# A retention layer and a squared-ReLU FFN on one core: every engine's row of operations written down

## The chip, the core and the metric

One core of a Trainium2 chip runs the whole kernel in one launch. Time is device microseconds (us) of that core. Five engines with queues of their own work side by side: TensorE (PE, matmuls), VectorE (DVE), ScalarE (ACT), GpSimd (POOL) and SyncE (SP, which here only issues DMAs). Each takes its instructions strictly in the order in which they were put into its queue.

## What is computed

```python
gamma = 1.0 - 2.0 ** (-5.0 - np.arange(H))          # q, k, v: (4, 8, 768, 64)
for t in range(S):
    state = gamma * state + outer(k[:, :, t], v[:, :, t])
    y[:, :, t] = (1 / sqrt(64)) * q[:, :, t] @ state
x = y.transpose(0, 2, 1, 3).reshape(3072, 512)
h = np.maximum(x @ w_in, 0.0)                       # w_in (512, 2048)
out = (h * h) @ w_out                               # w_out (2048, 512), out (3072, 512)
```

Inputs and output are float32; the kernel's matmuls run in bf16.

## The kernel before

The 3072 tokens are 24 chunks of 128. Everything that the kernel does is written down as an *operation* with a name: `Plan.add` collects the name, the engine or engines that may do it, an assumed duration, and what it reads and writes. `Plan.schedule` then replays the operations on an assumed clock and returns one sequence; the instructions are put into the engines' queues in that sequence. So `schedule` decides the order on each queue, which of the four PSUM tiles (`fps`, here called banks) a group takes, and which of two `r` buffers a ReLU takes. No time of that replay is a measurement.

The operations, by name:

- `ldk m`, `ldq m`, `ldv m`: load of chunk m (chunks 0 to 3 in pairs, `TWIN`), SP. `ldwin n`, `ldwout n`: slices of the weights, SP. They land in float32 in four slots each.
- `ck m`, `cq m`, `cv m`, `cwin j.c`, `cwout j.c`: casts to bf16 (lines 518, 520, 522 by engine; cv multiplies by decay factors, line 728). ck, cq and the weight casts may run on ACT, DVE or POOL.
- `X m`: for chunks from 7 on, a transposing DMA of casted q and k into `qkT` (line 761), SP. For earlier chunks `Tk m`, `Tq m` transpose on PE into a bank and `Ek m`, `Eq m` read it out; chunk 6 is flipped inside a visit and read out by `E6`.
- `A`, `B`, `C`: scores, state sums, and values for the first four chunks in pairs. `V m.n`: a *visit*, the values of chunk m and the scores and sums of chunk n in one block of matmuls (lines 787 to 824); `V.5` has scores alone, `V4.` values alone. After it DVE makes `P n` (masked scores), `S n.0`, `S n.1` (states) and `Y m` (the FFN's input, `xt`). The scores of V m.n need X n.
- `F1.b.f`: first FFN product of block b (one or two chunks; `BLOCKS`), a group of matmuls into one bank (line 936). `R b.f` is its ReLU on ACT (line 943), which frees the bank; `Q b.f` its square, on ACT (line 950) or DVE (line 952).
- Second product: for chunks 0 to 3 plain, `F2.c.j` (line 1108), read out by `O c` on ACT, stored by `st c`. For chunks 4 to 23 in pairs c, c+1, by seven products instead of eight (Strassen's way): DVE makes sums of h (here `S1`, `S2`, `S5`, `S6`, `S7` with the pair's number) and of w_out (`WT i`), PE the products `M1.c` to `M7.c` (line 1032), and `e4`, `cc` (ACT), `t1`, `u1`, `w`, `c` (DVE, line 1050) put them together; the last pair has `c1`, `c2` in place of `c`. Two stores, `st c.1` (cc) and `st c.0` (w and c's tile), line 1084; the last pair has three, lines 1075 and 1077.

What sets the order before: at each step `schedule` takes, of all operations that could start on any engine, the one with the least key.

```python
                    key = (t, o["prio"], i)
                    if best is None or key < best[0]:
                        best = (key, i, eng)
```

`prio` comes from formulas (`urgency(m)`, `LAGS`, `WPRIO`, `dma_order`) or from the table `RANK`, the engine for many operations from the table `HOME`. All stores but st22.0 go to SP.

The queues that came out of this, from the first FFN product to the tenth chunk and at the end:

```
PE   ... B3 F1.0.0 F1.0.2 C2.0 C2.1 F1.0.4 Tq4 F1.1.0 F1.0.6 F1.1.2 F1.1.4 F1.1.6 F1.0.8 Tk4 F1.0.10 F1.1.8 F1.1.10
     V.4 F1.0.12 F1.0.14 F1.1.12 V4. F2.0.0 Tq5 F1.1.14 F1.2.0 F2.0.1 Tk5 F1.2.4 F1.2.8 F2.0.2 F2.1.0 F1.2.12 F2.1.1
     F2.1.2 F2.0.3 F2.1.3 V.5 F2.2.0 F2.2.1 F2.3.0 F2.3.1 V5.6 F2.2.2 F2.2.3 F1.3.0 F1.3.4 F1.3.8 V6.7 F1.3.12
     F2.3.2 F2.3.3 M3.4 V7.8 M4.4 ... M3.22 M4.22 M6.20 M7.20 M1.22 M5.22 M2.22 M7.22 M6.22
SP   ... ldwin5 ldv4 ldwout0 ldq5 ldwout1 ldk5 ldwout2 ldwout3 ldq6 ldv5 ldk6 ldv6 ldq7 ldk7 ldv7 ldk8 ldq8 st0 st1
     X7 ldv8 ldk9 X8 st2 ldq9 ldv9 ldk10 ldq10 ldv10 st3 X9 ...
ACT  ... cwin0.0 cwin0.2 cwin1.0 R0.0 cwin2.2 Q0.0 R0.2 Q0.2 cwin3.2 R0.4 R1.0 Q1.0 cwin4.3 R0.6 R1.2 Q0.6 R1.4 R0.8 ...
```

Of the kernel before, what the change touches and what calls it, by code (L numbers as in the profile page):

```python
# [11 lines left out]
BF16 = mybir.dt.bfloat16  # L12
# [6 lines left out]
class Plan:  # L19
# [14 lines left out]
    HOP = 0.15  # L34

# [5 lines left out]
    def add(self, name, eng, dur, reads=(), writes=(), fn=None, prio=0.0, lat=0.0, bank=None, after=(), count=0, slot=None, lock=()):  # L41
# [19 lines left out]
        if name in HOME:  # L61
            eng = {HOME[name]: eng[HOME[name]]}
        prio = RANK.get(name, prio)
        self.ops.append(dict(i=i, name=name, eng=eng, flex=flex, deps=sorted(deps), fn=fn,
                             prio=prio, lat=lat, bank=bank, count=count, slot=slot, lock=lock))
        return i

    def schedule(self, nbanks, max_open, nslots):
# [12 lines left out]
        for o in ops:  # L81
            for e in o["eng"]:
                eng_free.setdefault(e, 0.0)
                pool.setdefault(e, set())
                if left[o["i"]] == 0:
                    pool[e].add(o["i"])
# [15 lines left out]
        while done < n:  # L102
            best = None
            for eng, cand in pool.items():
                ef = eng_free[eng]
                for i in cand:
# [17 lines left out]
                    key = (t, o["prio"], i)  # L124
                    if best is None or key < best[0]:
                        best = (key, i, eng)
            assert best is not None, "no operation can be placed"
            (t, _, _), i, eng = best
            o = ops[i]
            for e in o["eng"]:  # L130
                pool[e].discard(i)
# [34 lines left out]
            else:  # L166
                if eng == "PE":
# [21 lines left out]
                    if any(before < x <= issued for x in range(self.BLOCK0 - self.AHEAD, issued + 1, self.BLOCK)):  # L189
# [14 lines left out]
                end[i] = t + dur + o["lat"]  # L204
# [15 lines left out]
            for u in users[i]:  # L220
                same = list(ops[u]["eng"]) == [eng] and not move
                ready_at[u] = max(ready_at[u], start[i] + dur if same else end[i] + self.HOP)
                left[u] -= 1
                if left[u] == 0:
                    for e in ops[u]["eng"]:
                        pool[e].add(u)
# [11 lines left out]
AHEAD = 4  # L238
WARM = 20.0
FILL = 0.215  # L240
WARMING = 18.4
PACE = 8
LEAD = 2
# [5 lines left out]
CVT = {'DVE': 0.69, 'POOL': 1.07}  # L249
TCAST = {'DVE': 0.43, 'ACT': 0.63, 'POOL': 0.64}  # L250
TEVAC = {'ACT': 0.6, 'DVE': 0.62}
NPAIR = 2
F2LAG = 3.5
F2WAIT = 4
LAST = [256, 128, 128]
CAST = {"k": {"DVE": 0.43, "ACT": 0.63, "POOL": 0.64}, "q": {"DVE": 0.43, "ACT": 0.63, "POOL": 0.64}}
WCAST = {"DVE": 0.43, "ACT": 0.63, "POOL": 0.64}
EVAC = {"ACT": 0.6, "DVE": 0.62}
WPRIO = {"in": -2.0, "out": 2.0, "sum": 3.0}
# [3 lines left out]
SQUARE = {"DVE": 0.7, "ACT": 0.63}  # L263
WSUM = {"DVE": 0.69}
ASUM = {"DVE": 0.69}
LAGS = {
    16: 4.0, 4: 10.75, 6: 18.25, 10: 2.25, 20: 1.75, 14: 3.0, 8: 2.25, 18: 3.0, 12: 1.75, 22: 2.0,
}
RELU = {"ACT": 0.6}
# [4 lines left out]
PAIRS_A = {"S1": ((0, 0), (1, 1), ALU.add, None), "S5": ((0, 0), (0, 1), ALU.add, None),  # L274
           "S2": ((1, 0), (1, 1), ALU.add, None), "S6": ((1, 0), (0, 0), ALU.subtract, (1, 0)),
           "S7": ((0, 1), (1, 1), ALU.subtract, (0, 1))}
HOME = {
    'cwin4.1': 'POOL', 'ck0.1': 'ACT', 'Eq2.0': 'ACT', 'cwout2.1': 'ACT', 'cwin4.2': 'DVE', 'cwout3.0': 'DVE',
    'S5.18': 'DVE', 'R12.14': 'ACT', 'R1.10': 'ACT', 'Q8.10': 'DVE', 'R6.0': 'ACT', 'ck10': 'POOL', 'R6.14': 'ACT',
    'Q9.4': 'ACT', 'ck20': 'POOL', 'cq13': 'POOL', 'Q10.14': 'ACT', 'R4.8': 'ACT', 'R11.0': 'ACT', 'R3.12': 'ACT',  # L280
    'R4.14': 'ACT', 'cq2.1': 'DVE', 'cwin5.0': 'DVE', 'Q4.2': 'ACT', 'Ek2.0': 'ACT', 'ck21': 'POOL', 'Q8.6': 'ACT',
    'S7.20': 'DVE', 'Q11.6': 'ACT', 'Q10.10': 'DVE', 'Ek2.1': 'DVE', 'cq16': 'ACT', 'R1.8': 'ACT', 'S2.4': 'DVE',
    'WT7.0': 'DVE', 'Q12.6': 'DVE', 'Q2.8': 'ACT', 'Q6.2': 'ACT', 'R0.10': 'ACT', 'cq9': 'POOL', 'Q3.4': 'ACT',
    'R7.4': 'ACT', 'ck11': 'DVE', 'R8.0': 'ACT', 'Q5.2': 'ACT', 'R7.10': 'ACT', 'ck15': 'POOL', 'S2.20': 'DVE',
    'R7.12': 'ACT', 'cq5': 'ACT', 'Q7.6': 'DVE', 'ck5': 'DVE', 'ck4': 'POOL', 'cwin0.2': 'ACT', 'Q10.8': 'DVE',
    'Q7.4': 'DVE', 'R3.4': 'ACT', 'Q7.14': 'ACT', 'R4.10': 'ACT', 'R8.6': 'ACT', 'WT7.1': 'DVE', 'R9.6': 'ACT',
    'Ek4': 'DVE', 'S2.6': 'DVE', 'Q4.14': 'ACT', 'cv2.1': 'DVE', 'R6.6': 'ACT', 'Q7.12': 'DVE', 'cwout1.1': 'POOL',
    'Q12.0': 'ACT', 'S6.6': 'DVE', 'Q7.0': 'ACT', 'cwin3.2': 'ACT', 'S2.12': 'DVE', 'S5.22': 'DVE', 'Ek0.1': 'DVE',
    'Q0.0': 'ACT', 'cq17': 'ACT', 'S1.22': 'DVE', 'R7.14': 'ACT', 'cq18': 'POOL', 'S7.18': 'DVE', 'R9.12': 'ACT',
    'S2.14': 'DVE', 'R6.4': 'ACT', 'R3.8': 'ACT', 'Q6.0': 'ACT', 'R0.6': 'ACT', 'cq0.0': 'ACT', 'R4.0': 'ACT',  # L290
    'cq0.1': 'POOL', 'R0.14': 'ACT', 'S6.16': 'DVE', 'cwin5.3': 'ACT', 'S7.4': 'DVE', 'R5.12': 'ACT', 'S7.16': 'DVE',
    'ck22': 'POOL', 'S1.6': 'DVE', 'Q1.8': 'ACT', 'Eq0.0': 'DVE', 'R5.10': 'ACT', 'ck8': 'ACT', 'Q9.10': 'ACT',
    'R8.10': 'ACT', 'cq22': 'POOL', 'S2.18': 'DVE', 'Q6.4': 'DVE', 'R11.14': 'ACT', 'Q9.12': 'DVE', 'Q3.12': 'DVE',
    'cq4': 'POOL', 'ck2.0': 'ACT', 'cwout1.3': 'POOL', 'R7.8': 'ACT', 'Q9.6': 'ACT', 'R10.2': 'ACT', 'WT4.1': 'DVE',
    'Eq2.1': 'ACT', 'Q11.2': 'DVE', 'Q7.2': 'ACT', 'cq19': 'POOL', 'R11.8': 'ACT', 'Q7.8': 'DVE', 'S6.22': 'DVE',
    'S7.14': 'DVE', 'Q3.0': 'ACT', 'Q11.10': 'DVE', 'cwin1.2': 'POOL', 'S0': 'ACT', 'R9.10': 'ACT', 'Q9.8': 'DVE',
    'ck9': 'POOL', 'cwin3.0': 'POOL', 'Q0.6': 'ACT', 'Ek0.0': 'DVE', 'R5.14': 'ACT', 'S6.4': 'DVE', 'Q5.6': 'DVE',
    'cwout1.0': 'DVE', 'R9.0': 'ACT', 'Eq5': 'DVE', 'R8.14': 'ACT', 'S1.8': 'DVE', 'S7.12': 'DVE', 'S7.6': 'DVE',
    'R6.10': 'ACT', 'R12.6': 'ACT', 'cwin2.2': 'ACT', 'R4.12': 'ACT', 'cwout2.2': 'POOL', 'Q8.4': 'ACT',
    'Q11.0': 'ACT', 'R10.14': 'ACT', 'Q5.10': 'ACT', 'R10.12': 'ACT', 'cwout0.0': 'DVE', 'S2.22': 'DVE',  # L300
    'R10.10': 'ACT', 'R11.12': 'ACT', 'Q10.0': 'ACT', 'Q11.12': 'DVE', 'cq21': 'POOL', 'S5.12': 'DVE', 'R8.2': 'ACT',
    'Q0.8': 'ACT', 'Q6.6': 'ACT', 'Q5.8': 'ACT', 'R2.8': 'ACT', 'S6.12': 'DVE', 'R7.6': 'ACT', 'Q7.10': 'ACT',
    'cwin4.3': 'ACT', 'Q0.14': 'DVE', 'R1.14': 'ACT', 'cwout3.3': 'ACT', 'R9.4': 'ACT', 'Q5.4': 'ACT', 'S6.18': 'DVE',
# [33 lines left out]
    'R11.0': 16.0, 'M2.4': 73.143, 'Q0.8': 4.0, 'M5.6': 89.857, 'R0.14': 2.75, 'Q5.6': 12.75, 'M5.16': 162.857,  # L337
    'V10.11': 63, 'X11': 1.5, 'S21.1': 17.0, 't1.18': 27.0, 'cq8': -11.0,
}
ORDER = (  # L340
    "k0 q0 v0 q2 k2 v2 i0 i1 i2 q4 i3 i4 k4 i5 v4 o0 q5 o1 k5 o2 o3 q6 v5 k6 v6 q7 k7 v7"
)

# [9 lines left out]
def kernel(  # L353
# [638 lines left out]
    def products(c0):  # L992
# [31 lines left out]
        def product(i, bank, half, bank_use):  # L1024
# [13 lines left out]
            if first:  # L1038
                op["op"] = pl.ops[k]
# [168 lines left out]
```

## Time and profile before

| what | us |
|---|---|
| three runs | 203.77, 204.69, 204.86; median 204.69 |
| the profiled execution: span from first to last instruction | 202.7 |
| what lies around the span, by the runs | 1.1 to 2.2 |
| PE busy, DVE busy, ACT busy, POOL busy | 192.8, 150.0, 130.3, 31.3 |
| first FFN product starts | 17.54 |
| visit V7.8 starts | 62.42 |
| last matmul group ends | 198.94 |
| granted TensorE clock | 1.00 in every slice |

The profiled execution has no run time of its own, so its span stands beside the runs. The profile has a page (busy shares, forty slices of the span, DMA queues, the chain of work that ended last, the costliest groups, the DMA issues) and views of the trace behind it: a timeline by engine, lists of waits, and the chain in order of time. A matmul row's length is modelled and overlaps the next; the distance from one group's start to the next is its pace.

### The profile page before, as it was taken

To read this page: it belongs to the slowest core of one execution; us is meant where nothing else is said; L and a number is where in the kernel's file an instruction comes from. 1 tells how busy PE (TensorE), PEld (TensorE's weight loads), DVE (VectorE), ACT (ScalarE), POOL (GpSimd) and SP (SyncE) were. 2 spreads that over 40 slices of the span, in tenths; PEclk is the share of its full clock that TensorE was granted. 3 is DMA by queue.
4 is the path that set the end of the run, shared out by engine and by line. 5 is a ranking of instruction groups with operands and counts; after the bars stand their busy time and mean duration, and the time that the engine had idled before them with its cause. 6 is when DMAs were issued, how large, how long until landed. Compare 5 with 4: busy or idle time off the path is not lost.

```text
span 202.7 us, 7020 instructions
## 1 busy us (share of the span) xinstructions
PE 192.8 (95%) x3032; PEld 159.4 (79%) x3032; DVE 150.0 (74%) x283; ACT 130.3 (64%) x229; POOL 31.3 (15%) x56
## 2 busy tenths in 40 slices
PE   8886999899989999999999999999999999999992
PEld 6554887664577888888888888888888888888881
DVE  3486449569849988969898888878998784934762
ACT  8565888788871883787975485569375873835210
POOL 6541252220102101310211012203010000000000
PEclk9999999999999999999999999999999999999999
DMA  5999999999999999999999999999676100111313
GB/s 159 290 314 320 348 344 330 361 246 210 236 191 219 231 247 212 205 234 186 148 240 165 261 211 218 178 222 194 143 145 97 48 17 3 52 52 55 102 55 105
DMA packets 97935, 38.46 MB, mean 190 GB/s; under 512 B 81008, under 2 KB 94320, under 8 KB 97904
## 3 DMA queue, kind: packets, MB, share of 16 engines
q1 hardware_dynamic: 97760, 37.89, 86.2%
q8 instruction: 23, 0.38, 0.8%
q10 hardware_dynamic: 144, 0.13, 0.2%
q14 instruction: 8, 0.07, 0.1%
HBM read 27.26 MB, written 6.29 MB: 166 GB/s over the span
## 4 chain that ended last, share of the span: by engine, by line
PE 75%; DMA 15%; SPq 5%; POOL 1%; DVE 1%; issue 1%; ACT 0%; DVEq 0%
PE fps L936 33%; PE fps L1032 29%; DMA kn<-in_k_dram 8%; PE fps L1108 6%; DMA wst<-in_moe_w_in_dram 4%; DMA qkT<-kqs 3%; SPq L910 3%; PE yy L787 2%; SPq L537 2%; PE yy L802 1%; PE sc L813 1%; PE sc L824 1%; POOL w_in L522 1%; DVE wu L1050 1%; POOL h L522 0%
## 5 line engine op out<-in xcount | busy, mean ns | idle before, releaser
L936 PE MATMUL fps<-xt,w_in 128*128 128x256 bf16 (+1 forms) x832 | 94.0, 264 | 1.6 <-ACT w_in L518 1.2
L936 PEld LDWEIGHTS <-w_in 128*128 128x128 bf16 x832 | 74.8, 98 | 11.5 <-ACT w_in L518 2.0
L943 ACT ACTIVATE r<-fps 128x512 f32<-128x512 f32 x96 | 56.4, 592 | 34.6 <-PE fps L936 28.6
L950 ACT ACTIVATE h<-r 128x512 bf16<-128x512 f32 x63 | 39.1, 627 | 1.4
L1032 PE MATMUL fps<-wst,h 128*128 128x256 bf16 x320 | 39.4, 273 | 0.0
L1032 PEld LDWEIGHTS <-h 128*128 128x128 bf16 x320 | 31.0, 98 | 3.9
L952 DVE TENSOR_TENSOR h<-r 128x512 bf16<-128x512 f32 x33 | 22.8, 705 | 8.7 <-ACT r L943 8.6
L1032 PEld LDWEIGHTS <-wst 128*128 128x128 bf16 x240 | 23.3, 98 | 2.8
L1007 DVE TENSOR_TENSOR wst<-h 128x1024 bf16<-128x1024 bf16 x30 | 19.4, 685 | 2.9 <-ACT h L950 2.6
L1032 PE MATMUL fps<-w_out,wst 128*128 128x256 bf16 x160 | 20.3, 273 | 0.0
L728 DVE TENSOR_TENSOR vs<-vn,vf 128x512 bf16<-128x512 f32 x20 | 13.8, 691 | 6.3 <-DMA vn<-in_v_dram 6.3
L889 DVE TENSOR_TENSOR xt<-yy,yf 128x512 bf16<-128x512 f32 x20 | 13.7, 687 | 3.5 <-PE yy L802 3.4
L522 POOL CAST kqs<-kn 128x512 bf16<-128x512 f32 x12 | 8.0, 666 | 51.0 <-DMA kn<-in_k_dram 32.3
L1108 PE MATMUL fps<-w_out,h 128*128 128x512 bf16 x64 | 15.0, 379 | 0.7 <-DVE w_out L520 0.7
L1007 DVE TENSOR_TENSOR h<-h 128x1024 bf16<-128x1024 bf16 x20 | 14.0, 729 | 0.2
L880 DVE TENSOR_TENSOR state<-sc,state 128x256 bf16<-128x256 f32 x33 | 13.8, 418 | 0.5
L867 DVE TENSOR_TENSOR pt<-sc,cmask 128x512 bf16<-128x512 f32 x20 | 13.6, 681 | 0.0
L522 POOL CAST kqs<-qn 128x512 bf16<-128x512 f32 x11 | 6.9, 626 | 42.9 <-DMA qn<-in_q_dram 30.6
L1050 DVE TENSOR_TENSOR wu<-fps,wu 128x512 f32<-128x512 f32 (+1 forms) x16 | 9.1, 572 | 5.0 <-ACT osb L1060 2.8
L1108 PEld LDWEIGHTS <-h 128*128 128x128 bf16 x64 | 5.9, 98 | 6.8 <-issue 0.8
L1060 ACT ACTIVATE osb<-fps 128x512 f32<-128x512 f32 x10 | 5.9, 594 | 8.3 <-PE fps L1032 8.3
L1050 DVE TENSOR_TENSOR osb<-fps,osb 128x512 f32<-128x512 f32 (+1 forms) x15 | 9.0, 601 | 2.6 <-PE fps L1032 1.7
(85 smaller groups left out, 173.4 us busy)
## 6 DMA issues: line engine op xcount, KB each, us to landing
qn<-in_q_dram SPq DMA_DIRECT2D x20, 256.0 KB, 5.1
kn<-in_k_dram SPq DMA_DIRECT2D x20, 256.0 KB, 5.6
vn<-in_v_dram SPq DMA_DIRECT2D x20, 256.0 KB, 5.2
out_dram<-osb SPq DMA_DIRECT2D x19, 256.0 KB, 3.3
wst<-in_moe_w_out_dram SPq DMA_DIRECT2D x4, 1024.0 KB, 10.1
wst<-in_moe_w_in_dram SPq DMA_DIRECT2D x4, 512.0 KB, 8.4
wst<-in_moe_w_in_dram SPq DMA_DIRECT2D x2, 1024.0 KB, 8.3
kn<-in_k_dram SPq DMA_DIRECT2D x2, 512.0 KB, 4.3
```

Source lines behind the costliest of these rows:

```text
L522: nc.gpsimd.tensor_copy(o, t)
L728: lambda: nc.vector.tensor_tensor(out=o[:], in0=t.rearrange("s (h d) -> s h d", h=H), in1=vf[:, i, :, None].to_broadcast([P, H, D]), op=AL ...
L880: f = lambda cc=cc, j1=j1, j0=j0: nc.vector.tensor_tensor(out=sts[j1][:], in0=cc, in1=sts[j0][:], op=ALU.add)
L889: lambda: nc.vector.tensor_tensor(out=xt[:, :, u * C : u * C + C].rearrange("s p (g t) -> s g p t", g=2), in0=yy[:, :, 0:256].rearrange("s ...
L936: nc.tensor.matmul(ps[:, u * n : u * n + n], lhsT=w_in_bf[j][:, cb, c * P : (c + 1) * P], rhs=xt[:, cb, cols], start=(cb == 0), stop=(cb = ...
L943: nc.scalar.activation(o, t, AF.Relu)
L950: nc.scalar.activation(hv, rv, AF.Square)
L952: (nc.vector if on == "DVE" else nc.gpsimd).tensor_tensor(out=hv, in0=rv, in1=rv, op=ALU.mult)
L1007: lambda on, o=a[name], x=a[x], y=a[y], op=op: (nc.vector if on == "DVE" else nc.gpsimd).tensor_tensor(out=o, in0=x, in1=y, op=op), prio=c ...
L1032: nc.tensor.matmul(ps[:, 256 * half : 256 * half + 256], lhsT=a[left][:, f], rhs=right(f), start=(first and f == 0), stop=True, skip_group ...
L1050: return lambda ps: nc.vector.tensor_tensor(out=o, in0=ps[:, lo:hi], in1=y, op=op)
L1108: nc.tensor.matmul(ps[:, 0:w], lhsT=h2[:, fb, u * C : u * C + C], rhs=w_out_bf[j][:, c, ns], start=(fb == 0), stop=(fb == NFB - 1))
```

## The change

The tables `HOME`, `RANK` and `ORDER`, `LAGS`, and all `prio` arguments go. A new table `TURNS` holds, for every engine, the full row of operation names, and `schedule` may place only the next name of a row; it still chooses banks and buffers on its assumed clock. The assumed durations are other numbers (they shape banks, buffers and the count of warming matmuls alone, as rows and engines are fixed). In front of F1.0.0 the rows are nearly those of before; from there on they differ on all engines. The sums of h are now called H1, H2, H5, H6, H7. A unit's stores may go to SP or ACT, as the row has them. `after=` adds two conditions to the replay (a group of h may open only after the second product that reads the buffer's old content has opened; a unit's bank after the unit before it), which need no instruction. `FUSED` is empty and `DOUBLE` is 24, the number of chunks: the new branches `relu_square` and `visit2` with two chunks make nothing, except that V23. is written by `visit2`, with the same matmuls. The arithmetic is the same.

```diff
-        if name in HOME:
-            eng = {HOME[name]: eng[HOME[name]]}
-        prio = RANK.get(name, prio)
...
+        known = {o["name"]: o["i"] for o in ops}
+        turns = {e: [known[x] for x in TURNS[e].split()] for e in pool}
+        assert sorted(i for x in turns.values() for i in x) == list(range(n))
+        for e, x in turns.items():
+            for i in x:
+                ops[i]["eng"] = {e: ops[i]["eng"][e]}
+        at = dict.fromkeys(pool, 0)
+
+        def offer():
+            for e, x in turns.items():
+                if at[e] < len(x) and left[x[at[e]]] == 0:
+                    pool[e].add(x[at[e]])
...
-                    key = (t, o["prio"], i)
-                    if best is None or key < best[0]:
-                        best = (key, i, eng)
+                    if best is None or t < best[0]:
+                        best = (t, i, eng)
...
+TURNS = {
+    "POOL": (
+        "iota3 ident iota iota2 cmask2 cmask ck0.0 cq0.1 cv0.0 cv0.1 ck2.1 cv2.0 cwin2.0 cwin2.2 cwin4.3 cwin5.0 "
+        "cwin5.2 cwout0.2 cwout0.3 cwout1.1 ck5 cwout2.1 cq5 cwout3.2 ck6 cq7 cq10 cq12 ck11 ck12 cq14 ck13 ck14 "
...
+    "DVE": (
+        "lng lnt ex2_f ex_f vf2 vf Ek0.0 Ek0.1 Eq0.0 P0.10 P0.01 P0.00 P0.11 S1 cq2.1 Y0.0 Y0.1 Ek2.1 P2.01 P2.00 "
+        "cv2.1 cwin0.2 P2.11 S2 P2.10 S3 Y2.0 cq4 Y2.1 cwin3.0 cwin3.2 Q0.2 Eq4 Q0.4 cwin4.2 cwin4.0 Q0.6 ck4 "
+        "Q1.2 Ek4 Q1.0 cv4 S4.0 Q0.14 S4.1 P4 cwout0.0 Q0.8 Q1.12 Y4 cwout1.3 cwout1.2 Q1.14 cwout2.3 cv5 Ek5 "
+        "WT7.0 WT4.0 WT1.0 cwout3.3 Q2.8 WT1.1 WT4.1 S5.0 WT3.0 P5 cv6 WT6.0 Y5 S6.0 P6 S6.1 cv7 WT7.1 S7.0 H5.4 "
+        "cv8 S7.1 Y6 P7 WT3.1 WT6.1 Y7 H1.4 cv9 ck9 S8.0 H7.4 Q4.10 P8 ck10 t1.4 H2.4 S8.1 H6.4 cv10 u1.4 Y8 H1.6 "
...
+        "Y15 c.8 S16.0 cv17 P16 S16.1 ck20 H1.12 H5.12 H7.12 P17 S17.0 H7.10 Y16 cv18 Q8.4 H2.12 S18.0 Y17 cv19 "
+        "S18.1 u1.10 P18 w.10 S19.0 cv21 P19 H1.14 cv20 cq21 S19.1 H5.14 Y18 H2.14 c.10 H6.12 Y19 S20.0 cv22 P20 "
...
+        "t1.20 u1.20 H1.22 H5.22 H7.22 H2.22 w.20 H6.22 t1.22 c.20 u1.22 w.22 c2.22 c1.22 "
+    ),
+    "ACT": (
+        "vf20 vf0 yf0 yf1 yf2 yf3 ck0.1 cq0.0 Eq0.1 cq2.0 S0 Eq2.0 ck2.0 Ek2.0 Eq2.1 cwin0.0 cwin1.2 cwin1.0 R0.0 "
+        "Q0.0 R0.2 R0.4 R1.4 Q1.4 cwin4.1 R0.6 R1.6 Q1.6 R1.2 R1.0 cwin5.3 cwin5.1 R1.10 Q1.10 R0.10 Q0.10 R0.14 "
+        "R1.8 Q1.8 R0.8 cwout0.1 R1.12 R0.12 cwout1.0 Q0.12 R1.14 R2.0 R2.12 cwout2.2 Q2.12 cwout2.0 R2.8 "
+        "cwout3.0 cwout3.1 cq6 R2.4 Eq5 Q2.4 ck7 E6 O1 cq8 O0 Q2.0 ck8 O2 O3 R3.8 Q3.8 R3.0 R3.12 Q3.12 cq9 Q3.0 "
+        "R3.4 e4.4 Q3.4 R4.4 Q4.4 R4.10 R4.6 R4.0 Q4.0 Q4.6 R4.12 Q4.12 R4.2 Q4.2 R4.14 R4.8 Q4.8 Q4.14 cc.4 cq11 "
+        "e4.6 st4.0 R5.2 R5.12 Q5.12 Q5.2 R5.8 cc.6 R5.4 Q5.4 cq13 R5.14 R5.10 Q5.14 Q5.10 R5.6 R5.0 Q5.0 R6.0 "
...
+        "Q12.10 cc.16 R12.8 Q12.8 e4.18 R12.0 Q12.0 R12.14 Q12.14 cc.18 st18.1 e4.20 R12.12 Q12.12 cc.20 e4.22 "
+        "cc.22 st22.0 "
+    ),
+    "SP": (
+        "ldk0 ldq0 ldv0 ldq2 ldk2 ldv2 ldwin0 ldwin1 ldwin2 ldq4 ldwin3 ldwin4 ldk4 ldwin5 ldv4 ldk5 ldwout0 "
+        "ldwout1 ldv5 ldwout2 ldq5 ldwout3 ldq6 ldk6 ldk7 ldq7 ldq8 ldv6 ldk8 ldv7 X7 ldv8 st0 ldq9 X8 ldv9 ldk9 "
+        "ldk10 ldq10 st3 st2 ldv10 ldq12 X9 ldq11 ldk11 X10 ldv11 st1 ldv12 ldk12 X11 ldq14 ldk13 ldq13 X12 ldk14 "
...
+    "PE": (
+        "Tk0.0 Tk0.1 Tq0.1 Tq0.0 A0.1 A0.0 B0 B1 Tq2.0 C0.0 C0.1 Tk2.0 Tk2.1 Tq2.1 A2.0 A2.1 B2 B3 F1.0.0 C2.0 "
+        "C2.1 F1.0.2 F1.0.4 Tq4 F1.1.4 F1.1.6 F1.0.6 F1.1.2 F1.1.0 F1.0.10 Tk4 F1.1.10 F1.1.8 F1.0.8 F1.0.14 V.4 "
+        "F1.1.12 F1.1.14 F1.0.12 V4. F2.1.0 F2.0.0 F1.2.0 F1.2.12 Tk5 F2.0.1 F2.1.1 F1.2.8 F1.2.4 F2.1.2 F2.0.2 "
+        "Tq5 F2.0.3 F2.1.3 V.5 F2.2.0 F2.3.0 F2.2.1 F2.2.2 V5.6 F2.3.1 F2.2.3 F2.3.2 F1.3.0 V6.7 F2.3.3 F1.3.8 "
+        "F1.3.12 F1.3.4 V7.8 M3.4 M4.4 F1.4.4 F1.4.10 F1.4.6 F1.4.0 F1.4.14 F1.4.12 F1.4.2 M5.4 F1.4.8 M1.4 V8.9 "
...
+        "M7.8 F1.7.14 F1.8.14 F1.8.10 F1.8.0 F1.8.4 V16.17 F1.8.12 F1.8.8 F1.8.2 F1.8.6 M5.10 V17.18 M1.10 M2.10 "
+        "F1.9.0 F1.9.14 V18.19 F1.9.2 F1.9.4 F1.9.12 F1.9.6 M6.10 M7.10 F1.9.8 M3.12 V19.20 M4.12 F1.9.10 "
...
+        "M3.22 M4.22 M6.20 M7.20 M5.22 M2.22 M1.22 M6.22 M7.22 "
...
-            pl.add(f"st{c0}.{x}", "SP", STORE, k, (),
-                   lambda t=t, dst=dst: nc.sync.dma_start(dst, t[:].rearrange("p (i n) -> p i n", i=2)), prio=-1)
+            pl.add(f"st{c0}.{x}", {"SP": STORE, "ACT": STORE}, 0.0, k, (),
+                   lambda on, t=t, dst=dst: (nc.sync if on == "SP" else nc.scalar).dma_start(
+                       dst, t[:].rearrange("p (i n) -> p i n", i=2)))
```

On ACT's row stand st4.0, st4.1, st6.1, st8.1, st10.1, st12.0, st18.1 and, as before, st22.0; the other stores are on SP's.

## What I predict

> **What bounds the kernel.** First the page's busy shares and its slices.
>
> ```profile
> PE 192.8 (95%) x3032; PEld 159.4 (79%) x3032; DVE 150.0 (74%) x283; ACT 130.3 (64%) x229; POOL 31.3 (15%) x56
> ...
> PE   8886999899989999999999999999999999999992
> ...
> DMA  5999999999999999999999999999676100111313
> ```
>
> TensorE (PE) is the bound, and its clock is 1.00 throughout. Before slice 13 (62 us) the DMA engines are full too. A full PE digit is not a full PE, so I counted work. Rows of the chain of waits give the paces: a product or an FFN1 group of 8 matmuls 0.87, four FFN2 matmuls 0.86, a one-chunk FFN1 group 0.90, a visit 0.66, the two C visits 0.8, a transposing group 0.24. From F1.0.0 (17.54) to V7.8 (62.42) the order of before holds 16 x 0.874 + 8 x 0.90 + 16 x 0.866 + one product 0.87 + 0.8 + 4 x 0.24 + five visits 3.2 = 40.9, and 44.9 passed: **4.0 us lost**. After that some 2 us are spread over 137 us, and the waits list for PE names none above 0.1 there. The largest losses, from the timeline of PE:
>
> ```profile
> 17.54 1.35 PE L936 MATMUL fps<-xt,w_in 128*128 128x256 bf16 x8 [1.03 <-ACT w_in L518]
> 19.05 1.05 PE L936 MATMUL fps<-xt,w_in 128*128 128x256 bf16 x8 [0.16 <-ACT w_in L518]
> 39.05 1.02 PE L1108 MATMUL fps<-w_out,h 128*128 128x512 bf16 x4 [0.68 <-DVE w_out L520]
> 58.39 0.32 PE L813 MATMUL sc<-qkT 64*64 64x64 bf16 x16 [0.53 <-DMA qkT<-kqs]
> ```
>
> F1.0.0 and F1.0.2 wait for weight casts, F2.0.1 for a slice of w_out, V6.7 for transposing DMA X7. Then the chain of waits, in order of time:
>
> ```profile
> 55.79 7.04 DMA qkT<-kqs
> 62.83 0.04 issue
> 62.87 0.32 PE sc L813 x16
> ```
>
> X8 lands at 62.83, just as V7.8's scores need it: PE idles hardly at all, yet this transfer ends last. Last the tail, from the timeline:
>
> ```profile
> 197.03 1.91 PE L1032 MATMUL fps<-wst,h 128*128 128x256 bf16 x16
> 197.23 0.60 ACT L1060 ACTIVATE osb<-fps 128x512 f32<-128x512 f32 x1 [3.98 <-PE fps L1032]
> 197.86 1.55 DVE L1050 TENSOR_TENSOR wu<-fps,wu 128x512 f32<-128x512 f32 x3 [1.95 <-ACT osb L1060]
> 199.11 0.69 ACTq L1077 DMA_DIRECT2D out_dram<-wu  x1
> 199.44 0.34 SPq L1077 DMA_DIRECT2D out_dram<-wu  x1
> ```
>
> **Part 1: casts and FFN1, to V.5.** The built programs hold the same PE work in another order (two or three warming matmuls more). What I assume: weight slices land as in before, for up to w_in the loads stand in the same order. The first casts of the slices start at 16.86, 18.36, 19.90, 22.57, 25.39 and 29.31.
>
> cwin0.2 moves from ACT (where it ended 18.01) to DVE (0.42, free at 16.9): F1.0.0 runs unbroken, 17.54 to 18.45. C2.0 and C2.1 follow and end 19.8; F1.0.2 to 20.7; F1.0.4 needs two POOL casts of the slice of 19.90 (0.61 each, to 21.1) and ends 21.8, against 22.24: 0.44 gained. cq4 now stands on DVE between Y2.0 and Y2.1 and waits for its load (21.01, as POOL's cast did); Y2.1 still ends at 22.0, in time for F1.1.4 at 22.05.
>
> Then the waits that ACT's new row adds. cwin4.1 waits for 25.39; behind it stand R0.6, R1.6, Q1.6, R1.2, at 0.5 apart: R1.2 ends 28.05, and F1.1.10, which takes its bank, starts 0.25 late. cwin5.3 and cwin5.1 wait for 29.31 and end 30.4; R1.10 behind them ends 30.97, and F1.0.14 takes its bank: 0.3 lost. V.4, F1.1.12, F1.1.14, F1.0.12, V4. follow to 35.75. Before stood at 35.16 here without F1.1.14 (0.87): 0.28 gained.
>
> The load of k5 now goes ahead of the first slice of w_out, which lands near 34.1 instead of 33.2; its four casts are done at 35.4, before F2.1.0 at 35.75. cwout1.0 on ACT waits for the second slice (37.06 as before); R1.14 behind it ends 38.75, so F1.2.12 starts 0.4 late. F2.0.1 comes at 39.95, long after its slice: before's 0.68 is gone. The fourth slice has one load more ahead of it (q5) and lands near 44.6; F2.0.3, at 45.45, loses 0.1. q6 lands 45.7, and cq6, R2.4, Eq5 on ACT end at 47.25. **V.5 starts at 47.35, against 48.12 with the same work done: 0.77 gained.**
>
> **Part 2: X7 and X8.** The queue delivers in order; the starts of the casts that waited for a load show it:
>
> ```profile
> 54.07 0.63 ACT L518 ACTIVATE kqs<-qn 128x512 bf16<-128x512 f32 x1 [0.38 <-DMA qn<-in_q_dram]
> ...
> 59.40 0.69 DVE L728 TENSOR_TENSOR vs<-vn,vf 128x512 bf16<-128x512 f32 x1 [2.96 <-DMA vn<-in_v_dram]
> ...
> 60.63 0.61 POOL L522 CAST kqs<-kn 128x512 bf16<-128x512 f32 x1 [9.10 <-DMA kn<-in_k_dram]
> ```
>
> q8 at 54.07, X7 at 58.39 with st0 and st1 ahead of it, v8 59.40, k9 60.63, X8 62.83. So X8 alone took 2.2, two stores and X7 4.32: a store 1.05, a load 1.1. In the new SP row the same eleven loads precede X7, but no store; X7 lands at 54.07 + 2.25 = 56.3. V6.7 wants it at 56.05 (V.5, four F2, V5.6, three F2, F1.3.0 after 47.35): 0.25 lost. Then v8, st0, q9, X8: one store fewer than before, so X8 lands 1.05 earlier, at 61.75. PE would be at V7.8's scores at 60.55. **X8 gates: 1.2 us of wait.** The new order has M3.4 behind V7.8 (before had it ahead), 0.87 that is still to do. Net: 62.87 - 61.75 - 0.87 = **0.25 gained**. So most of part 1 is given back here.
>
> **Part 3: V7.8 to the end of PE.** Nothing of before can be won here. Could something be lost? For each PE group I took the PE work between it and what it waits for, less the durations of the operations in that chain, queue neighbours included. In before the least are about 0.6; in the new order eight are thinner: M4.4, F1.5.2, V18.19 (0.24), F1.9.0, F1.11.6 (0.3), F1.11.12, M5.22, M7.22 (0.2). None is negative: 0. Upward the bound is a DVE pair that takes 1.69 (34.07, beside POOL casts) where it takes 1.29 alone (31.03): 0.4 at V18.19 and F1.11.6, less their margins, 0.25. V18.19 by hand: four groups and a visit, 4.16, against visit result 0.9 and S18.0, Y17, cv19, S18.1, u1.10, P18 = 3.0. Transposing DMAs have casts ready 8 us or more ahead of their visit; the X rows take 3.3 to 7.0 to land. Casts moved between DVE, ACT and POOL and eight squares moved from DVE to ACT lie beside PE: DVE's sum falls by 1 us, ACT's rises by under 1. Stores st4.0 to st18.1 leave SP for ACT; the only row of an ACT issue is 0.69, so 7 x 0.69 = 4.8 on an engine that idles 50 us after 62; put into the chains above they thin none of the eight. SP loses stores at its head that blocked later loads: 0, as no visit after 62.87 waits for a load.
>
> **Part 4: the tail.** Before, DVE's last step ends 0.47 after PE (199.41), SP issues its store in 0.34. In the new order M2.22 and M1.22 come earlier, cc.22 and w.22 finish under PE, but the last product is M7.22, so c1 ends 0.47 after PE just the same, and its store is ACT's. By the row of 0.69 that is 0.35 later; but half of that row ran beside SP's own issue, so it may be 0. I take 0.17.
>
> [...]
>
> **Sum.** -0.25 + 0.17 = -0.08. The profiled execution has a span of 202.7; the runs (203.77 to 204.86, median 204.69) lie 1.1 to 2.2 above it, what surrounds the span. Nothing around it changes, so I take the difference from the median: **204.6**, own range 203.7 to 205.5 (0.9 of new waits in part 1 that may not come or may double, and the thin chains).
>
> **Rivals.**
> A, X8 is not the gate. For it: part 1 leans on landings that vary (loads 3.6 to 9.0 us), and if k8 and q9 land early X8 does too. Against: the DMA engines are full until 62, so X8 lands earlier only by what no longer stands ahead of it. Then V7.8 starts at 60.1: 62.42 - 0.87 - 60.1 = 1.45 gained, less 0.17: 203.4. With also the 0.95 of new waits in part 1 gone, 202.5. Chance 0.33.
> B, slower: a store holds SP's queue ahead of X8. The new SP row has st0 between v8 and q9, and st0 waits for O0, which on ACT stands behind ck7, E6, O1 and cq8, so behind V.5 and the load of q8. For it: stores do hold that queue in before, as SP's own waits list shows (in all, times, longest):
>
> ```profile
> SPq L1084 <- ACT osb L1060: 22.3, 5, 13.4
> ```
>
> Against: by my times O0 ends at 51.1 and SP reaches st0 near 53. It decides from 53 on, us for us, as q9 and X8 cannot be issued; from 54.05 X8 lands no earlier than before, and the sum is 0.87 + 0.17 = 1.04: 205.7; each further us adds one. Chance 0.22.
> That the change does not do what it says is excluded: in the order of the built program each queue holds its written row. The forecast, X8 as the gate, keeps 0.45.
>
> A run of this kernel tells about 0.5% (1.0 us) from no change. Faster by more: rival A, 0.33. Within: 0.45. Slower: rival B, 0.22. The range reaches into both: 202.9 to 205.8.
>
> **What would show it.** V.5 near 47.4 and F2.0.1 without a wait: part 1. A PE wait of about 1 us on qkT at the second visit after it: part 2; if V7.8's scores start by 60.6, rival A. If SP stands at st0 and X8 lands after 62.8: rival B. PE waits on DVE of 0.1 to 0.3 after 62 would be the thin chains of part 3. A last ACT issue of 0.3 or 0.7: the tail. I am wrong if weight slices land a us off, or if the ACT queue holds a new wait above 1 us.

## The result, and the profile after

Four runs of the changed kernel took 210.87, 212.91, 213.15 and 213.15 us, median 213.03; the kernel before, beside it, had a median of 204.23. Here and below a median is over all runs, and a ratio is of means without the runs that fell in a slower state, as 3 of the 23 of before beside e10 did (206.8 to 207.6, median 204.13). The ratio is 1.041, with a 95% interval of 1.036 to 1.046: **8.8 us slower**, where 204.6 was forecast. The profiled span is 211.3, against 202.7.

The page of the changed kernel, busy shares and slices (40 slices of 5.3 us):

```profile
PE 194.7 (92%) x3029; PEld 160.4 (76%) x3034; DVE 147.7 (70%) x285; ACT 128.6 (61%) x230; POOL 31.1 (15%) x53
...
PE   8878999989999999999998999990899999999993
...
PEclk9999999999999999999999999998599999999999
```

One slice has no PE at all, another a granted clock of 0.5 beside it. Both are new. So the loss sits near 140 to 150 us, not in the stretch up to V7.8 on which the forecast spent most of its work. The waits list of the changed kernel (engine and line, what ended the wait, us in total, times, longest) names who waited:

```profile
ACT e L1103 <- DMA out_dram<-wu: 8.1, 1, 8.1
...
PE fps L975 <- ACT r L982: 6.8, 3, 6.4
...
ACT r L982 <- DMA out_dram<-wu: 2.9, 1, 2.9
```

ACT starts an evacuation `e4` only after a *store to the output* has landed. No e4 needs a store. What needs one must stand ahead of it in ACT's queue. The chain of waits of the changed kernel, in order of time, shows what that is:

```profile
144.43 2.88 DMA out_dram<-wu
...
147.39 0.38 ACTq L1133
...
147.81 0.09 ACT e L1103
...
148.09 0.60 ACT r L982
...
148.74 3.57 PE fps L975 x16
```

Read it downwards. SP issues st10.0 at 144.43, and it lands at 147.31. Only then does ACT issue st10.1, the other store of the same unit, and behind st10.1 in ACT's row stand e4.12 and R9.10. st10.0 comes late because the transpose X21 stands ahead of it on SP (timeline of SP):

```profile
140.07 4.26 SPq L740 DMA_TRANSPOSE qkT<-kqs  x1
```

X21's issue alone holds SP for 4.26 us, at a place where the page's DMA row stands at 9; the other transposes of this kernel take 1.3 to 4.0. X21 was not waiting for a cast: that of its q had ended at 136.26, that of its k at 138.86, and DVE had finished the data of st10.0 at 138.98. (Further back the chain view puts the end of a POOL cast at 142.15 inside this issue. That is the cast of k22, which X21 does not need.) Why this issue is the longest is open.

ACT had finished what came before at 139.70; PE, with no bank free, stopped at 142.36. PE's timeline:

```profile
139.57 2.78 PE L975 MATMUL fps<-xt,w_in 128*128 128x256 bf16 x24
148.74 3.57 PE L975 MATMUL fps<-xt,w_in 128*128 128x256 bf16 x16 [6.38 <-ACT r L982]
152.10 1.45 PE L1078 MATMUL fps<-w_out,wst 128*128 128x256 bf16 x8
```

16 matmuls take 3.36 to the next group where 16 normally take 1.75, and the eight after them 1.29 (the group behind starts at 153.39) where 0.87 is usual. The windows view of the first of these stretches (bounds; busy time and instructions of PE, PEld, DVE, ACT, POOL; granted clock; DMA share; GB/s) shows why:

```profile
148.70:152.10 3.40, 3.36 (x16) 2.38 (x16) 0.98 (x2) 2.59 (x5) 0.00 (x0) 0.50 0.48 111
```

So the idle is followed by half a clock (0.68 in the 1.3 us after): 6.38 idle plus (3.36 - 1.75) + (1.29 - 0.87) = 2.03 for the clock, 8.4 in one place. The 2.9 us of ACT from 108.6 to 111.5 are the same thing in small: st6.1 waits for st6.0 (on SP from 106.19, landed 111.0), and PE loses 0.62. Together 9.0, more than the difference of the spans, 8.6. A third wait of the kind, 2.3 us at st12.0 for st12.1 (160.7 to 163.0), costs PE nothing.

The built program of the changed kernel says what this issue waits for. In it the 118 DMAs of both queues add to eight completion semaphores ("lanes", DMAHW0 to DMAHW7) in turn, in the order of the program. The issue of st10.1 has a wait for the DMA that last held its lane, and one for the unit's first store. (The two stores of a unit write interleaved pieces of the output, two blocks of 128 rows by 256 columns each, crosswise, which is taken for the reason of the second wait.)

```
179 L1133 DMACopy out_0_dram<-osb1_114 128x2x256 [waits DMAHW4_49,DMAHW0_49]
```

That is st10.1: DMAHW4 is st10.0's lane, DMAHW0 its own. The last DMA on its own lane, a load of k, had landed at 141.42, so here the partner decided: st10.0 lands at 147.31, and the issue starts at 147.39, 0.08 later.

**Theory L**: a store on ACT waits at its issue for another DMA (its partner or its lane), and everything behind it on ACT waits too. **Rival R**: the new rows are themselves worse behind V7.8. **Rival C**: the price is the seven issues on ACT.

### The profile page after: what moved, and what is told of

The parts are those of the page before. It is cut to its first block, busy times and chain, and to the rows that moved or that the text cites. A ratio compares the mean times of both kernels' runs of the same rounds, so it can differ in the third digit from the quotient of the medians.

```text
span 211.3 us, 7012 instructions
## 1 busy us (share of the span) xinstructions
PE 194.7 (92%) x3029; PEld 160.4 (76%) x3034; DVE 147.7 (70%) x285; ACT 128.6 (61%) x230; POOL 31.1 (15%) x53
## 4 chain that ended last, share of the span: by engine, by line
PE 48%; DMA 23%; SPq 14%; DVE 7%; issue 3%; POOL 2%; ACT 1%; ACTq 0%; DVEq 0%; POOLq 0%
PE fps L1078 23%; PE fps L975 18%; DMA kn<-in_k_dram 13%; SPq L698 6%; SPq L950 4%; DMA out_dram<-wu 4%; PE fps L1158 3%; DMA qn<-in_q_dram 3%; DMA vn<-in_v_dram 3%; DVE wst L1053 2%; SPq L740 2%; SPq L533 2%; PE yy L764 1%; DVE wu L1099 1%; PE yy L779 1%
## 5 line engine op out<-in xcount | busy, mean ns | idle before, releaser
L975 PEld LDWEIGHTS <-w_in 128*128 128x128 bf16 x832 | 76.0, 99 | 19.4 <-issue 8.1
L982 ACT ACTIVATE r<-fps 128x512 f32<-128x512 f32 x96 | 55.3, 591 | 36.4 <-PE fps L975 25.3
L994 ACT ACTIVATE h<-r 128x512 bf16<-128x512 f32 x71 | 43.3, 627 | 1.3
L1078 PE MATMUL fps<-wst,h 128*128 128x256 bf16 x320 | 38.6, 273 | 0.6 <-ACT r L982 0.6
L1053 DVE TENSOR_TENSOR wst<-h 128x1024 bf16<-128x1024 bf16 x30 | 20.6, 698 | 3.6 <-PE fps L1078 3.6
L996 DVE TENSOR_TENSOR h<-r 128x512 bf16<-128x512 f32 x25 | 17.7, 710 | 5.3 <-ACT r L982 5.3
L518 POOL CAST kqs<-qn 128x512 bf16<-128x512 f32 x11 | 8.2, 749 | 58.3 <-DMA qn<-in_q_dram 58.3
L708 DVE TENSOR_TENSOR vs<-vn,vf 128x512 bf16<-128x512 f32 x20 | 14.6, 731 | 2.8 <-DMA vn<-in_v_dram 2.8
L863 DVE TENSOR_TENSOR xt<-yy,yf 128x512 bf16<-128x512 f32 x19 | 13.0, 686 | 3.8 <-PE yy L779 3.8
L1103 ACT ACTIVATE e<-fps 128x256 f32<-128x256 f32 x10 | 3.8, 381 | 13.8 <-DMA out_dram<-wu 8.1
```

The lines of the kernel that those rows point to most:

```text
L518: nc.gpsimd.tensor_copy(o, t)
L708: lambda: nc.vector.tensor_tensor(out=o[:], in0=t.rearrange("s (h d) -> s h d", h=H), in1=vf[:, i, :, None].to_broadcast([P, H, D]), op=AL ...
L975: nc.tensor.matmul(ps[:, u * n : u * n + n], lhsT=w_in_bf[j][:, cb, c * P : (c + 1) * P], rhs=xt[:, cb, cols], start=(cb == 0), stop=(cb = ...
L982: nc.scalar.activation(o, t, AF.Relu)
L994: nc.scalar.activation(hv, rv, AF.Square)
L996: (nc.vector if on == "DVE" else nc.gpsimd).tensor_tensor(out=hv, in0=rv, in1=rv, op=ALU.mult)
```

## Experiments

All times are medians; each ratio is to the kernel before on the same chip, whose own median lay between 204.04 and 204.40.

| kernel | us | ratio, 95% |
|---|---|---|
| changed | 213.03 | 1.041 (1.036 to 1.046) |
| e1_all_sp | 207.29 | 1.015 (1.007 to 1.022) |
| e2_later | 207.08 | 1.014 (1.009 to 1.019) |
| e3_split10_12 | 212.32 | 1.040 (1.035 to 1.045) |
| e4_split8_10_12 | 212.01 | 1.039 (1.034 to 1.044) |
| e5_sp_written_late | 207.96 | 1.017 (1.012 to 1.021) |
| e6_before_act_stores | 204.94 | 1.003 (1.000 to 1.006) |
| e7_before_sp_late | 204.75 | 1.001 (0.999 to 1.003) |
| e8_later_two | 207.58 | 1.014 (1.009 to 1.019) |
| e9_st10_ahead_of_x21 | 212.27 | 1.038 (1.032 to 1.044) |
| e10_after_no_stores | 204.30 | 1.001 (0.999 to 1.003) |
| e11_before_no_stores | 204.23 | 1.000 (0.998 to 1.003) |
| e12_first_stores | 205.40 | 1.004 (1.000 to 1.007) |

### e1_all_sp: the seven stores back on SP

```diff
-ACT ... e4.6 st4.0 R5.2 ... R6.8 st4.1 R6.10 ... Q7.6 st6.1 R7.0 ... Q9.6 st8.1 R9.8 Q9.8 st10.1 e4.12
-    ... cc.12 st12.0 R10.4 ... cc.18 st18.1 e4.20 ...
+ACT ... the same row without them
+SP  ... X12 st4.0 ... X13 st4.1 ... X16 st6.1 ... X19 st8.1 ... X22 st10.1 X23 st12.1 st12.0 ... st18.1 st18.0 ...
```

> The changed kernel with its seven unit stores (st4.0, st4.1, st6.1, st8.1, st10.1, st12.0, st18.1) taken from ScalarE's row and put into SyncE's, each behind a transpose or the other store of its unit; every other row unchanged. Theory W (a store at the head of ScalarE's queue waits for another DMA, and the evacuations behind it stop TensorE): ScalarE's waits of 2.9 us and 8.1 us for 'DMA out_dram' are gone, TensorE's 0.6 and 6.4 us with them, and the granted clock stays near 1.00, which gives back another 2 us; span about 211.3 - 0.6 - 6.4 - 2.1 = 202.2, time about 203.9 (203 to 205.5). Rival R (the new rows are themselves worse behind V7.8: thinner chains of evacuation): the waits for DMA go, but TensorE stops elsewhere; 208 or more. Rival C (the price is the seven issues on ScalarE): at 0.38 us each 2.7 us less, about 210.

Measured: 207.29, span 205.4, outside what L allowed. ACT's waits for the output are gone, the idle of 6.4 and the half clock too, so 5.7 of 8.8 us come back. C is out: it allowed 2.7. But L had expected 203.9, and 3 us stay. The timeline of PE shows new stops:

```profile
116.32 0.32 PE L789 MATMUL sc<-qkT 64*64 64x64 bf16 x16 [0.87 <-DMA qkT<-kqs]
...
140.67 0.32 PE L763 MATMUL yy<-pt,vs 64*64 64x64 bf16 x16 [1.39 <-DVE xt L862]
```

In the first line a transpose is late, with stores ahead of it on SP; in the second a step of DVE, which stands behind a cast of q whose load landed at 138.59. Whether stores on SP or the rows make these stops is left to later kernels.

### e2_later: on ACT, but later

```diff
-ACT ... Q7.6 st6.1 R7.0 ... Q9.8 st10.1 e4.12 ... cc.12 st12.0 R10.4 ... R11.0 cc.14 ...
+ACT ... Q7.6 R7.0 ... Q7.14 st6.1 ... Q9.8 e4.12 ... cc.12 R10.4 ... R11.0 st10.1 st12.0 cc.14 ...
```

> All seven stores stay on ScalarE, but st6.1 stands 12 operations later in its row and st10.1 and st12.0 some 20 and 10 later, directly ahead of cc.14, which needs the buffer of st10.1. Theory W: st6.1 then finds st6.0 landed and does not wait; st10.1 comes some 12 us of ScalarE's work later than it did and finds st10.0 landed if SyncE's own row is not later than now; time 203.9 to 205.5, with at most 1 us of wait at a store. Rival R: 208 or more, TensorE idle outside the stores. Rival C: as the changed kernel less nothing, since all seven issues are still there: 213.

Measured: 207.08, span 205.1, a miss by 1.6 us. The wait of 8.1 us is gone with the stores still on ACT. But st6.1 found another DMA to wait for, a load of k that had nothing to do with it. ACT's timeline, then PE's:

```profile
122.39 0.60 ACT L980 ACTIVATE r<-fps 128x512 f32<-128x512 f32 x1 [3.07 <-DMA kn<-in_k_dram]
```

```profile
123.04 1.03 PE L973 MATMUL fps<-xt,w_in 128*128 128x256 bf16 x8 [1.66 <-ACT r L980]
```

st6.0 had been issued at 106.72, 15.2 us ahead of st6.1 (121.89); what is left is the lane, which in the built program a load of k held last. With 0.63 at the next group PE lost 2.3 us here; 205.1 less that would be 202.8.

### e3_split10_12 and e4_split8_10_12: partner or lane

The stores of units 10 and 12 (in the second kernel of unit 8 too) are written as two rectangles each, which don't overlap with the partner's:

```diff
+            if c0 in (10, 12):
+                def put(on, t=t, x=x):
+                    for i in range(2):
+                        col = 256 * (x ^ i)
+                        (nc.sync if on == "SP" else nc.scalar).dma_start(
+                            out[rows(c0) + i * C : rows(c0) + i * C + C, col : col + 256], t[:, 256 * i : 256 * i + 256])
```

> The rows as in the changed kernel. The stores of units 10 and 12 alone are each written as two rectangles (one block of 128 rows by 256 columns a DMA) in place of one DMA over two blocks, so that the ranges of a unit's two stores no longer interleave and the second need not wait for the first; four DMAs more in all. Theory W with the partner's landing as what is waited for: st10.1's wait of 8.1 us falls to under 1 us (what is left is the wait for the DMA eight issues earlier, long landed), TensorE's 6.4 us and the low clock go, st6.1's 2.9 us and TensorE's 0.6 stay; time 204 to 205.5. Rival L (what it waits for is the semaphore lane, shared with a DMA of SyncE eight issues earlier): in this kernel the lanes of st10.1 fall on loads that land early, so L expects the same; the next kernel tells W from L. Rival R: 208 or more.

> As the kernel with units 10 and 12 split, with unit 8 split too: two DMAs more ahead of unit 10 move the lanes on, so that the second half of st10.1 shares its semaphore lane with the transpose X21, which is issued on SyncE at 140.1 us and lands some 6 us later. Rival L (a DMA's issue also waits for the DMA that last held its lane): ScalarE stands at st10.1 for about 7 us, until X21 has landed at about 146, and the time is 211 to 213, as in the changed kernel, though the unit's stores no longer overlap. Theory W with the partner's landing alone: no wait, 204 to 205.5, as in the kernel before this one.

Measured: 212.32 and 212.01. In the first, the expectation fell: no overlap, and ACT still stands 6.5 us. The second came as theory L said. The chain of the first, and of the second:

```profile
139.08 7.01 DMA qn<-in_q_dram
...
146.11 0.36 ACTq L1134
```

```profile
139.60 6.52 DMA qkT<-kqs
...
146.14 0.34 ACTq L1134
```

The wait is now for whatever DMA holds the lane: a load of q in one, the transpose X21 in the other, as the shift of the lanes should make it. In the second X21 adds only the last 1.2 us; up to 144.90 a load of q held the lane of st10.1's first half, and earlier ACT stood 2.8 us at st8.1 for the lane of a load of v. The load of q was expected to have landed early; at this place, with the page's DMA row at 9, it takes 7.0 us. So partner (8.1 us in the changed kernel) and lane (6.5 in e3) each suffice. The lane wait is not one that the partner had hidden in the changed kernel, where st10.1's lane was free at 141.42: the added DMAs put st10.1 on other lanes.

### e5_sp_written_late: the same rows, another order of the program

Every engine's queue is the changed kernel's; only where SP's DMAs stand in the program among the others' operations differs, and so the lanes and which store of a pair waits for which.

```diff
-            for i in sequence:
+            waiting, order_ = [], []
+            for i in sequence:
+                if pl.on[i] == "SP":
+                    waiting.append(i)
+                    continue
+                need = [j for j, x in enumerate(waiting) if x in pl.ops[i]["deps"]]
+                if need:
+                    order_ += waiting[: need[-1] + 1]
+                    del waiting[: need[-1] + 1]
+                order_.append(i)
+            for i in order_ + waiting:
```

> Every engine's row as in the changed kernel, operation for operation, stores on ScalarE included. Only the program's order across engines is another: each DMA of SyncE is written down just ahead of the first operation of another engine that needs it, in place of at its planned time. So a store of ScalarE has fewer of SyncE's DMAs written ahead of it: the DMA eight issues earlier, whose semaphore lane it shares, is an older one, and of the pairs of units 6, 10 and 12 ScalarE's store is written first, so that SyncE waits for it and not the other way. Theory L (a DMA's issue waits for the DMA that holds its lane and for the unit's first store, and on ScalarE that stops the evacuations): ScalarE's waits for DMAs at stores fall from 2.9 and 8.1 us to under 1 each, TensorE's 0.6 and 6.4 go, the clock stays at 1.00; 203.5 to 205.5. Rival R (the rows themselves are worse behind V7.8): 207 or more, as with all stores on SyncE. Rival C (the seven issues on ScalarE): 213, since they are all where they were.

Measured: 207.96, span 206.0: by the time alone, rival R's range. But st6.1 is issued at 109.42 and st10.1 at 141.13, without the long waits on ACT, with all rows unchanged. So the idle of 6.4 us did not belong to the rows. The waits went to SP, and there they are not free either. SP's timeline and PE's:

```profile
106.74 0.89 SPq L696 DMA_DIRECT2D qn<-in_q_dram  x1
113.31 0.38 SPq L1131 DMA_DIRECT2D out_dram<-wu  x1
...
114.32 1.71 SPq L738 DMA_TRANSPOSE qkT<-kqs  x1
```

```profile
118.12 0.32 PE L788 MATMUL sc<-qkT 64*64 64x64 bf16 x16 [2.23 <-DMA qkT<-kqs]
```

st6.0, now written behind st6.1, holds SP for 5.7 us; the transpose behind it comes late, and PE stops for 2.2 us. An earlier transpose lands late at 102.78, 7.7 us after its issue, for another 1.0.

### e6_before_act_stores and e7_before_sp_late: the parts on the kernel before

```diff
+ON_ACT = ((4, 0), (4, 1), (6, 1), (8, 1), (10, 1), (12, 0), (18, 1))
+            q = nc.scalar if (c0, x) in ON_ACT else nc.sync
```

> The kernel before, its order of the program unchanged, with the same seven stores (st4.0, st4.1, st6.1, st8.1, st10.1, st12.0, st18.1) issued by ScalarE in place of SyncE. There, the DMAs that share their lanes were issued 10 us or more earlier (st10.1: lane of st8.0, issued at 113.0, ten us ahead of it), and five of the seven are their unit's first store. Theory L: no wait for a DMA of over 1 us on ScalarE, with st12.0, which waits for c.12 and for st12.1's landing, the one that may stand a few us; 204 to 206. Rival C (a store on ScalarE costs the evacuations behind it whatever it waits for): 206.5 or more.

> Control: the kernel before with its stores on SyncE and only the program's order across engines changed in the same way (each DMA of SyncE written just ahead of its first user). Theory L: a store waiting on SyncE held nothing up before, so nothing is to be gained: 203.6 to 204.8, the same as before. If the other order across engines helps in itself, 203 or less.

Measured: 204.94 and 204.75, both within 0.5% of before. The same seven stores on ACT in before's order cost nothing that this can tell: the only wait for the output in ACT's list is one of 0.4 us, and st12.0 stands 1.3 us (143.24 to 144.55) until st12.1 has landed, without a stop of PE. C is out here too. So with waits of 0.4 and 1.3 us the seven stores on ACT are harmless here (ratio 1.003, 1.000 to 1.006). And the other order of the program alone changes nothing that this can tell (1.001, 0.999 to 1.003).

### e9_st10_ahead_of_x21: the partner earlier

```diff
-SP  ... ldq22 ldq23 X21 st10.0 X22 ...
+SP  ... ldq22 ldq23 st10.0 X21 X22 ...
```

> The changed kernel with one swap in SyncE's row: st10.0 ahead of the transpose X21 and not behind it; st10.1 stays where it was on ScalarE. st10.0 is then issued at 140.1 and not at 144.4 and lands near 142.6 (2.5 to 3 us after issue). Theory L: ScalarE stands at st10.1 for about 3 us in place of 8.1; TensorE, which had 1.7 us in hand there (8.1 less 6.4), idles 1 to 1.5. If the fall of the granted clock needs a long idle of TensorE (4.5 us and more in three kernels so far, none at 1.7), the clock stays at 1.00 and the span is 211.3 - 5 - 2 = 204.3, time 206. If the clock falls with any idle at that place, 207.5 to 208.5.

Measured: 212.27; ACT still waits 8.0 us. The chain:

```profile
141.51 5.58 DMA out_dram<-wu
...
147.11 0.38 ACTq L1131
```

st10.0 is issued 2.9 us earlier and lands 0.2 earlier: with six loads right ahead of it, it takes 5.58 to land in place of 2.88. The expectation took the landing as fixed. PE idled 5.31 and the clock fell to 0.50 again, so a short idle at this place was not tried.

### e8_later_two: on ACT, later still

```diff
-ACT ... Q7.14 st6.1 ... R11.0 st10.1 st12.0 cc.14 ...
+ACT ... Q8.2 st6.1 ... R10.8 st10.1 cc.12 ... R11.14 st12.0 ...
```

(against e2_later)

> All seven stores on ScalarE as in the changed kernel; SyncE's row and every other row are the changed kernel's. Three stores stand later in ScalarE's row: st6.1 behind Q8.2, near 127 us, when st6.0 has landed and the DMA on its lane (st8.0, issued at 122.8 in the kernel with three stores later) too; st10.1 behind R10.8, near 154; st12.0 behind R11.14, near 160. Theory L: no wait for a DMA above 0.5 us at any store. The kernel with three stores later had a span of 205.1 with 2.3 us of TensorE waiting at st6.1; without them 202.8, time 204.4 (203.5 to 205.3), so the rows themselves cost nothing against the kernel before. Rival R (the rows are worse by 2 to 3 us, as the kernels with all stores on SyncE and with SyncE's DMAs written late could suggest): 206.5 or more, with TensorE waiting for transposes.

Measured: 207.58, a miss by 3 us and in rival R's range. The profiled run is the longest of the six (209.82). Its chain shows two waits for stores, one behind the other:

```profile
123.42 5.37 DMA out_dram<-osb
...
128.87 4.21 DMA out_dram<-osb
...
133.16 0.04 ACT osb L1107
```

st6.1 waits for its lane, which st8.0 on SP holds until 128.79; then takes 4.21 to land, and cc.10, which writes the buffer that st6.1 reads, waits for that. PE stops for 0.58, 1.05 and 1.82, and behind the last of these the granted clock falls (PE's timeline, then the windows view):

```profile
134.29 5.32 PE L973 MATMUL fps<-xt,w_in 128*128 128x256 bf16 x32 [1.82 <-ACT r L980]
```

```profile
134.20:139.60 5.40, 5.31 (x34) 4.05 (x34) 5.40 (x11) 3.42 (x7) 1.23 (x2) 0.68 1.43 174
```

These 32 matmuls take 5.16 where 3.5 is usual. Stops and clock together are 5.1, all of the span's excess (207.8 against 202.7). The fall is not in every run: three shorter ones (spans 204.6 to 205.6) have a mean clock of 0.998 to 1.000 against 0.992 here, a fourth (205.7) has 0.983. What the shorter runs lose by the stops is not shown. Later is not safe by itself.

### e10_after_no_stores and e11_before_no_stores: the rows alone

The ten stores of units 4, 6, 8, 10 and 12 are left out, so those rows of the output are not written.

```diff
+GONE = (4, 6, 8, 10, 12)
-                   lambda on, t=t, dst=dst: (nc.sync if on == "SP" else nc.scalar).dma_start(
+                   lambda on, t=t, dst=dst: None if c0 in GONE else (nc.sync if on == "SP" else nc.scalar).dma_start(
```

> The changed kernel without the ten stores of units 4, 6, 8, 10 and 12 (those rows of the output are not written), every other operation in its row. It shows what the new rows give when no store waits on any queue in the stretch from 70 to 165 us. Theory L (all that the change lost hangs on those stores): the wait of 8.1 us, TensorE's 7.0 us and the low clock go and no new wait comes: span 202.3 or a little less, time 203.9, and within 1 us of the kernel before without the same stores. Rival R (thin chains and late transposes in the new rows): 2 to 3 us more than the kernel before without the same stores, TensorE waiting for transposes or evacuations behind 100 us.

> The kernel before without the same ten stores. Its stores stood on SyncE and the profile shows TensorE waiting for nothing behind 62 us, so all theories expect 203.5 to 204.3, as with them; its use is as the mark for the changed kernel without stores.

Measured: 204.30 and 204.23. This settles R: without these stores the two orders take the same time, and behind V7.8 the changed one has no stop of PE that the timeline names. The place that cost 8.4 us now reads:

```profile
139.34 4.53 PE L976 MATMUL fps<-xt,w_in 128*128 128x256 bf16 x40
143.71 1.04 PE L1079 MATMUL fps<-w_out,wst 128*128 128x256 bf16 x8
```

The same 40 matmuls, 4.37 us to the next group; in the changed kernel 152.10 - 139.57 = 12.53. The whole loss hangs on these ten stores. For before they cost nothing (204.13 with them).

### e12_first_stores: all stores, where what they wait for is early

```diff
+ACT ... cc.4 st4.1 ... cc.6 st6.1 ... R9.14 st10.1 ... R11.14 st12.0 ...
+SP  ... X17 st8.1 ldk19 ...
```

> The changed kernel with all its stores again, five of the seven placed so that neither thing that a store was seen to wait for is late: st4.1 and st6.1 on ScalarE directly behind cc.4 and cc.6, as their units' first stores; st8.1 on SyncE behind X17, as its unit's first store; st10.1 on ScalarE behind R9.14, its unit's first store, with a lane last held by the load of v20 (issued near 127); st12.0 behind R11.14. All other rows are the changed kernel's. Theory L: no wait for a DMA above 1 us at a store on ScalarE and no clock loss, TensorE stops under 1 us in all behind 100 us; 204 to 205.3, level with the kernel before, and with the changed kernel without these stores (204.3). If stores in this stretch cost TensorE time wherever they stand (each occupies the DMA engines, which are full until about 147 us, so that the transposes behind come later), 206 to 207.5, as with the four placings so far, with TensorE waiting for transposes.

Measured: 205.40, span 204.3, no fall of the clock; L had allowed 205.3 and a wait of 1 us. Five stores moved, all of them kept: 7.6 of the 8.8 us are back. ACT waits 1.4 us at one store, st4.0, whose lane a load of q holds until 86.29. What is left of the timeline's stops behind 62 us:

```profile
90.32 0.32 PE L788 MATMUL sc<-qkT 64*64 64x64 bf16 x16 [0.66 <-DMA qkT<-kqs]
...
116.15 0.32 PE L788 MATMUL sc<-qkT 64*64 64x64 bf16 x16 [0.79 <-DMA qkT<-kqs]
```

1.45 of late transposes, about the 1.6 by which its span stands above that without the stores. No kernel tried here beats the one before.

## Why the prediction was wrong, point by point

- **What bounds it**: right. PE is the bound, and where nothing stops it both orders take the same time.
- **Part 1, V.5 at 47.35**: it came at 48.88, and before's was 48.12. F1.0.0 began at 17.70, F2.0.1's wait was gone as forecast, the waits behind R1.2 and R1.10 were 0.17 and 0.27. Two waits were missed. F1.2.4 waited 0.70 for Ek5, which stands on DVE behind cwout2.3 (41.83, when its slice had landed) and cv5, and so ran at 43.19. And V.5 waited 0.30 for the cast of k6 on POOL (47.96 to 48.83), whose load landed at 47.96. For both the row on its engine was in the diff; the chain was followed only for the casts of weights. The fourth slice of w_out also came 1.1 late (casts from 45.71 on, forecast 44.6); behind two of its casts ACT ended Eq5 at 48.42, so V.5 could not have come before that.
- **Part 2, X8 gates V7.8 at 61.75**: V7.8 came at 61.66, with no wait for qkT. The time was right by luck, through two errors of opposite sign: PE was 1.3 late (scores at 61.87, forecast ready at 60.55), and X8 landed 1.1 early (60.66). That is rival A's condition without its gain. With M3.4 still to do, 0.1 was lost up to here, not 0.25 gained.
- **Part 3, thin chains cost 0**: right (without the ten stores no stop). The stores are **the step that failed**: "7 x 0.69 = 4.8 on an engine that idles 50 us after 62". It priced what an issue *takes* (measured: 0.38 each) and put that into the chains. It did not ask what an issue *waits for*. The waits were 2.9 and 8.1 us, with 7.0 us of PE and 2.0 of clock behind them. In before, waits of this kind stood in the profile as SP's:

```profile
SPq L1084 <- DMA out_dram<-osb: 11.8, 6, 3.5
```

Rival B even read from the same list that a store holds the queue it stands in. Part 3 moved the stores to ACT and left their waits on SP. The prediction's own last condition (a new wait above 1 us in ACT's queue) is what came.
- **Part 4, the tail +0.17**: from the start of the last group of matmuls to the end it was 202.7 - 197.03 = 5.67 and is 211.3 - 206.22 = 5.08, so 0.59 shorter. c1 ends 2.37 after that start, as before (2.38), and ACT's last issue took 0.35 where SP's took 0.34. So the term is 0; the difference lies behind the last issue and was not looked into.
- **The seven issues themselves**: put on ACT in before's order they changed its time by a ratio of 1.003 (1.000 to 1.006). What counted in the changed kernel stood ahead of an issue: st10.0 lands at 147.31, ACT's semaphore instruction in front of st10.1 passes at 147.33, and the issue follows at 147.39 and takes 0.38. ACT's 8.1 us is that wait.
- **Rivals and range**: A's place was reached by other means, B (st0 ahead of X8) did not come. The right rival would have been "a store on ACT waits for its partner on SP, behind a transpose whose issue takes 4 us": 8 us if it comes, and nothing in the range allowed for it.

What stays open: how the microsecond (1.004, 1.000 to 1.007) that e12_first_stores still lacks divides between transposes delayed on SP's queue and transposes slowed by the stores on the DMA engines.

## What to carry to other kernels

Here the stores that went to ACT's queue took their waits along, 2.9 and 8.1 us in front of ACT's work, where their issues took 0.38 each. So before you price an issue, list what it waits for (data, the unit's other store, the lane), on which queue that stands, and what holds that queue. For two stores whose targets interleave, look at what stands behind the one that waits: both on SP's queue took 204.23 us in before's order and 207.29 in the new rows (e1_all_sp); with ACT's mostly first it was 205.40 in e12_first_stores and 207.96 in e5_sp_written_late, where st6.0 held SP for 5.7 us. Taking out the suspected DMAs altogether, with the output incomplete, separated their cost from that of the order around them (e10_after_no_stores: 204.30 in place of 213.03).

## What was not expected of the hardware

- **The clock after an idle.** After PE idles of 4.5, 5.3 and 6.4 us (e3, e9, the changed kernel) the granted clock was 0.50 for the next 3.4 us, after 5.1 (e4) 0.53 over 3.6. After 2.2 (e5) and 1.7 with 0.6 behind it (e2) it stayed at 1.00, but in the profiled run of e8 it fell too (0.68 over 5.4 us), after 1.05 and 1.82 with 2.4 us of work between them, and three other runs of e8 show hardly any fall (mean clock 0.998 to 1.000). So these rows give no least idle. By an estimate from the page's slices, the windows view and the paces of the groups, the clock fell 3.5 to 5.0 us into the idle in e3, e4 and the changed kernel, but 2.2 us into that of e9, and came back 3.3 to 5.8 us after the matmuls went on in these four.
- **How long a store takes to land**: 2.88 behind a transpose, 5.37 and 5.58 behind loads where the page's DMA row stands at 9, at the same size of 256 KB. A wait for a landing can't be taken from a median (2.2 for 12 of SP's stores in the changed kernel, most of which come after 160 us, where that row is at 3 or less).
- **An early clock.** Between 17.5 and 20 us the granted clock was 0.54 and 0.53 in the profiled executions of e1 and e4, and 1.00 in those of the changed kernel, e2 and e3, with the same order up to there. It costs little: e1's third group starts 1.4 us behind e2's (23.52 against 22.13), but its V.5 comes at 49.35 against 49.01, and e3's, at full clock, at 49.53.
